# u of a feed-forward tile transposed by a round trip through DRAM and 32x32 blocks, its second product two tiles behind

## The chip, the core and the metric

The kernel runs on one core of a Trainium2 chip, in one launch. The core has a matrix engine (TensorE, PE in the profile, with its weight loads as PEld), VectorE (DVE), ScalarE (ACT), GpSimd (POOL) and SyncE (SP, which issues transfers). Each engine works its own list of instructions in order, and they meet through semaphores. The time is device microseconds of one execution; what is compared is the median over several.

## The reference

```python
# attention, for each of 8 batches and 8 heads, 576 tokens of 64 features
q_d, k_d, v_d = means of q, k, v over groups of 4 tokens
out_up    = repeat(softmax(q_d k_d^T / 8) v_d, 4)
out_local = softmax(q k^T / 8 where |i - j| < 4) v
x = (out_up + out_local) as [4608 tokens, 512]

# feed-forward
h = x @ w_in                                   # [4608, 1024]
sm = exp(h - max(h)) / (sum(exp(h - max(h))) + 1e-9)
u = h * sm
ln = (u - mean(u)) / sqrt(var(u) + 1e-6) * g_ln
out = ln @ w_out                               # [4608, 512]
```

The weights are float64 and are brought to float32 on the chip. Each float32 factor of the feed-forward products is held as a rounded high part and a remainder, and a product is made of three: high by high, high by low, low by high.

## The kernel before

**Attention** is worked batch by batch, in nine items a batch: five `Local` items (two windows of 64 keys, all heads) and four `Pooled` ones (two heads each). An item has scores with a softmax, transposes, and an output that is added to `x`. The items' scores are written one item ahead.

**The feed-forward** works tiles of 128 tokens, 36 in all, a batch behind the attention. `split_x` makes the two parts of x. `ffn_in` multiplies by `w_in` into `h`, two PSUM banks that exist once (`ps_h`, one buffer), in 24 matmuls of 128x512 (L518); then come the row's maximum (DVE, L527), the exponential (ACT, L530), the product with h and its sum (DVE, L532), the mean (POOL, L536), its subtraction in place in `e` (ACT, L539), the sum of squares (ACT, L542), and the factor `s` of a row (POOL, L544 to L557). `ffn_out` takes the result, u, whose tokens lie on partitions: in two halves of four chunks, eight PE transposes of 128x128 bring the features onto partitions (L568, into a PSUM bank), ACT rounds the high part `uh` (L571), DVE subtracts for the remainder `ul` (L573), and 24 matmuls of 128x512 with `w_out` follow (L582). ACT scales the result (L588) and issues its store (L589). `uh` and `ul` have two buffers each, one tile's worth.

**The order.** `ffn_steps` gives the feed-forward in steps, four a tile, and each attention item takes two of them. A tile's second product stands behind the first product of the next tile. A tile waits in empty steps until the batch whose x it needs is finished (`xs`). From tile 31 on (`LAST`) no attention is left, and the transposes of the tile before are put between the two halves of a first product. A planner orders the instructions of each engine from estimated durations before the program is built, taking what is ready and earliest in the program; the result is a fixed list for each engine. Two exceptions stand in the program's own order: everything that SP issues, and PE's list in the last part.

**Loads on SP** are q and k of the next batch (32 transfers at an item's start, L111), v for the pooled sums (four a batch, L131, waited for by POOL at L278), and v's windows (20, L123). A transfer whose buffer is not yet free holds back everything that SP has after it.

**The first batch** is worked among the weights: `order` writes out the steps. A weight block goes through `f32` (one ACT and four DVE instructions, L178 to L189, in a buffer of tag `osb`) and `split` (L195, L196).

Of the kernel before, what the change touches and what calls it, by code (L numbers as in the profile page):

```python
# [11 lines left out]
F32 = mybir.dt.float32  # L12
# [8 lines left out]
# High words of the float64 numbers between which float32's normal ones lie, as float32.  # L21
# [5 lines left out]
def pooled_local_attention_then_solu_ffn(  # L27
# [11 lines left out]
    P = 128  # L39
# [14 lines left out]
    # Local windows: 64 consecutive keys each; window w serves queries [qlo, qhi).  # L54
# [4 lines left out]
    # Pooled query chunks, two heads of each side by side.  # L59
# [19 lines left out]
    for half in range(2):  # L79
        m = mask[half * W:(half + 1) * W, :]  # L80
        # keep 0 where |row - col| < FAC, else -1e9
# [11 lines left out]
    # k transposed, two heads by two, block diagonal: the other head's rows stay zero  # L93
# [4 lines left out]
    # pooled q, two heads by two, block diagonal too  # L98
# [4 lines left out]
    # Partition quadrant (par, dh) gets the tokens of a 32-token block of the heads of that  # L103
    # parity, half dh of the head's features, so that transposing 32x32 blocks leaves
    # features on partitions.
# [36 lines left out]
    # A float64 comes as two words. Its float32 bits: sign and top exponent bit, the  # L142
    # next 27 bits of the high word, the top 3 bits of the low word. The high word is
    # first held to the range of float32 (read as a float32, its order is that of |w|).
    class Weights:
# [25 lines left out]
        def f32(self):  # L171
# [4 lines left out]
            t = moe.tile([P, DO], F32, tag="osb", name=f"w32_{n}", bufs=3)  # L176
# [21 lines left out]
        def w_in(self):  # L198
            for cc in range(NCC):
                for n in range(2):  # L200
                    ns = slice(n * 512, n * 512 + 512)
                    self.split(self.f32(), wi_h[:, cc, ns], wi_l[:, cc, ns])
                    yield

        # the layer norm's g goes into w_out's rows
# [13 lines left out]
    class Batch:  # L219
        """What one batch's attention holds."""  # L220
# [15 lines left out]
        # q and k transposed, with their pooled sums (the means' factors are folded into  # L236
        # the scale and the weights)
# [6 lines left out]
        def pair(self, pr):  # L244
            kT = wk.tile([P, S], F32, tag="kT", name=f"kT_{self.b}_{pr}")
# [39 lines left out]
    class FirstBatch(Batch):  # L285
        """Leaves the transposes and the sums of v to the tensor engine."""
# [77 lines left out]
    # One item of attention: scores with their softmax, then the transposes, then the output.  # L364
    class Local:
        """Two windows of the local attention, all heads."""
# [64 lines left out]
    class Pooled:  # L431
        """The pooled attention of two heads."""
# [80 lines left out]
    def ffn_in(i, xh, xl):  # L513
# [25 lines left out]
        nc.scalar.activation(e, e, AF.Identity, bias=nmu, scale=1.0)  # L539
# [3 lines left out]
        # per-token factor: r / sqrt(r^2 * m2 / DFF + 1e-6), r = 1 / (sum + 1e-9)  # L543
# [17 lines left out]
    def ffn_out(i):  # L561
        u, s = done.pop(i)
        uts = []
        for g in range(2):
            tp = ps_t.tile([P, 4, P], F32, tag="t", name=f"ut_{i}_{g}")
            for j in range(4):
                fc = 4 * g + j
                nc.tensor.transpose(tp[:, j, :], u[:, fc * P:(fc + 1) * P], ident)  # L568
            uh = moe.tile([P, 4, P], F32R, tag="uh", name=f"uh_{i}_{g}", bufs=2)
            ul = moe.tile([P, 4, P], F32R, tag="ul", name=f"ul_{i}_{g}", bufs=2)  # L570
            nc.scalar.activation(uh, tp, AF.Copy)  # L571
            latest[:] = [
                nc.vector.tensor_tensor(out=ul, in0=tp, in1=uh.bitcast(F32), op=ALU.subtract)  # L573
            ]
            uts.append((uh, ul))
# [11 lines left out]
        osb = moe.tile([P, DO], F32, tag="osb", name=f"osb_{i}", bufs=3)  # L587
# [7 lines left out]
    # The tiles from which on the last batch's attention is over.  # L595
    LAST = ((B - 1) * S) // P

    # The feed-forward's chunks, each in two halves: its first product for a tile, then
    # its second one for the tile before.
    def ffn_steps():  # L600
        split = split_x(0)
        for i in range(NTILE + 1):
            if LAST <= i < NTILE:
                # no attention is left to fill the wait for the transposed u
                first, last = ffn_in(i, *split), ffn_out(i - 1)
                next(first)
                next(last)
                yield
                yield from first
                if i + 1 < NTILE:  # L610
                    split = split_x(i + 1)
                yield from last
                continue
            if i < NTILE:
                yield from ffn_in(i, *split)
                while i + 1 < NTILE and ((i + 2) * P - 1) // S not in xs:
                    yield
                if i + 1 < NTILE:
                    split = split_x(i + 1)
            if i > 0:  # L620
                yield from ffn_out(i - 1)
# [119 lines left out]
```

## Time and profile before

| What | Value |
|---|---|
| median of 3 runs | 697.27 us (695.83 to 699.69) |
| profiled execution, span from its first to its last instruction | 695.3 us |
| PE busy (matmuls) | 658.1 us, 95% of the span |
| DVE, ACT, POOL busy | 425.7, 388.6, 316.2 us |
| moved by transfers | 57.47 MB |
| transposes of u on PE (L568) | 288 |

The profile states no time for the profiled execution beyond its span; the span is 0.5 us below the fastest run and 2.0 us below the median. Times of PE matmuls overlap, since one starts before the last has drained: what a group costs PE is read from the starts, from its first instruction to the start of what follows. In a timeline a row gives start, duration, engine, line, operation, output and input, the count of merged instructions, and in brackets the engine's idle time before it with what ended that.

### The profile page before, as it was taken

To read this page: it belongs to the slowest core of one execution; us is meant where nothing else is said; L and a number is where in the kernel's file an instruction comes from. 1 tells how busy PE (TensorE), PEld (TensorE's weight loads), DVE (VectorE), ACT (ScalarE), POOL (GpSimd) and SP (SyncE) were. 2 spreads that over 40 slices of the span, in tenths; PEclk is the share of its full clock that TensorE was granted. 3 is DMA by queue.
4 is the path that set the end of the run, shared out by engine and by line. 5 is a ranking of instruction groups with operands and counts; after the bars stand their busy time and mean duration, and the time that the engine had idled before them with its cause. 6 is when DMAs were issued, how large, how long until landed. Compare 5 with 4: busy or idle time off the path is not lost. (4 is left out here: it accounts for less than half of the span.)

```text
span 695.3 us, 12961 instructions
## 1 busy us (share of the span) xinstructions
PE 658.1 (95%) x4880; PEld 522.8 (75%) x4880; DVE 425.7 (61%) x765; ACT 388.6 (56%) x784; POOL 316.2 (45%) x509
## 2 busy tenths in 40 slices
PE   3877799989999999999999999999999999999996
PEld 2666577868877788778877788778877788778885
DVE  4899999985377555765567655665567543333232
ACT  4645666854575466635765466634756465444533
POOL 3485468574723852248423842247443732222210
PEclk9975789999999999999999999999999999999999
DMA  9957526758427521085117411184130100000000
GB/s 171 211 179 147 121 82 134 158 118 145 104 55 131 115 51 47 23 141 116 49 32 133 118 47 47 25 145 110 49 83 16 33 17 16 16 31 16 15 31 30
DMA packets 203789, 57.47 MB, mean 83 GB/s; under 512 B 187856, under 2 KB 197072, under 8 KB 203728
## 3 DMA queue, kind: packets, MB, share of 16 engines
q1 hardware_dynamic: 198544, 47.22, 33.6%
q10 hardware_dynamic: 5184, 9.44, 3.6%
q8 instruction: 38, 0.62, 0.4%
q14 instruction: 23, 0.19, 0.1%
HBM read 47.19 MB, written 9.44 MB: 81 GB/s over the span
## 5 line engine op out<-in xcount | busy, mean ns | idle before, releaser
L582 PE MATMUL o<-wo_h,uh 128*128 128x512 f32 x288 | 118.3, 411 | 1.8 <-ACT uh L571 1.4
L518 PE MATMUL h<-wi_h,xh 128*128 128x512 f32 x288 | 119.5, 415 | 0.5 <-DVE e L532 0.5
L582 PE MATMUL o<-wo_l,uh 128*128 128x512 f32 x288 | 116.1, 403 | 0.4 <-POOL wo_l L196 0.4
L518 PE MATMUL h<-wi_l,xh 128*128 128x512 f32 x288 | 115.5, 401 | 0.0
L518 PE MATMUL h<-wi_h,xl 128*128 128x512 f32 x288 | 114.6, 398 | 0.1
L527 DVE TENSOR_REDUCE nmx<-h 128x1 f32<-128x1024 f32 x36 | 43.9, 1221 | 75.0 <-PE h L518 75.0
L582 PE MATMUL o<-wo_h,ul 128*128 128x512 f32 x288 | 81.6, 403 | 1.3 <-DVE ul L573 1.3
L507 POOL TENSOR_TENSOR xl<-x,xh 128x512 fp32r<-128x512 f32 (+1 forms) x40 | 47.2, 1185 | 75.4 <-PE ut L568 41.5
L573 DVE TENSOR_TENSOR ul<-ut,uh 128x512 fp32r<-128x512 f32 x72 | 48.4, 680 | 34.3 <-ACT uh L571 33.9
L582 PEld LDWEIGHTS o<-wo_h,uh 128*128 128x128 f32 x288 | 54.6, 190 | 16.1 <-issue 2.3
L518 PEld LDWEIGHTS h<-wi_h,xh 128*128 128x128 f32 x288 | 54.4, 189 | 13.8 <-issue 2.1
L518 PEld LDWEIGHTS h<-wi_h,xl 128*128 128x128 f32 x288 | 54.3, 189 | 13.0 <-issue 0.3
L582 PEld LDWEIGHTS o<-wo_l,uh 128*128 128x128 f32 x288 | 54.8, 190 | 11.4 <-POOL wo_l L196 0.5
L518 PEld LDWEIGHTS h<-wi_l,xh 128*128 128x128 f32 x288 | 54.4, 189 | 11.2 <-issue 0.9
L582 PEld LDWEIGHTS o<-wo_h,ul 128*128 128x128 f32 x288 | 52.4, 188 | 11.9 <-DVE ul L573 1.8
L378 PE MATMUL sc<-kbd,qT 128*64 128x128 f32 x640 | 52.4, 297 | 7.4 <-ACT kbd L250 6.4
L539 ACT ACTIVATE e<-e,nmu 128x1024 f32<-128x1024 f32 x36 | 41.4, 1150 | 29.9 <-POOL nmu L536 29.9
L530 ACT ACTIVATE e<-h,nmx 128x1024 f32<-128x1024 f32 x36 | 40.1, 1114 | 30.0 <-DVE nmx L527 30.0
L398 POOL TENSOR_TENSOR pl<-pl,rsl 128x512 f32<-128x512 f32 x40 | 44.7, 1119 | 20.9 <-DVE rsl L397 20.3
L389 POOL TENSOR_TENSOR pl<-pl,mxl 128x512 f32<-128x512 f32 x40 | 43.2, 1082 | 24.0 <-DVE mxl L388 20.9
L423 PEld LDWEIGHTS xp<-plT,vw 64*64 64x64 f32 x1280 | 43.5, 143 | 13.1 <-issue 4.8
L378 PEld LDWEIGHTS sc<-kbd,qT 128*64 128x64 f32 x640 | 38.8, 145 | 19.3 <-issue 7.4
(94 smaller groups left out, 1271.7 us busy)
## 6 DMA issues: line engine op xcount, KB each, us to landing
vw<-in_v_dram SPq DMA_DIRECT2D x160, 64.0 KB
vs<-in_v_dram SPq DMA_DIRECT2D x32, 288.0 KB
out_dram<-osb ACTq DMA_DIRECT2D x36, 256.0 KB
qm<-in_q_dram SPq DMA_DIRECT2D x112, 72.0 KB
km<-in_k_dram SPq DMA_DIRECT2D x112, 72.0 KB
stage<-in_moe_w_out_dram SPq DMA_DIRECT2D x8, 512.0 KB
stage<-in_moe_w_in_dram SPq DMA_DIRECT2D x4, 512.0 KB
w<-in_moe_w_in_dram SPq DMA_DIRECT2D x4, 512.0 KB
```

Source lines behind the costliest of these rows:

```text
L378: nc.tensor.matmul(sc[wi * W:(wi + 1) * W, 2 * pr:2 * pr + 2, :], bt.qT[:, pr, s0:s0 + W], kbd[:, pr, :, s0:s0 + W], start=True, stop=True,)
L389: nc.gpsimd.tensor_tensor(out=pl, in0=pl, in1=mx.unsqueeze(2).broadcast_to([P, H, W]), op=ALU.subtract)
L398: nc.gpsimd.tensor_tensor(out=pl, in0=pl, in1=rs.unsqueeze(2).broadcast_to([P, H, W]), op=ALU.mult)
L423: nc.tensor.matmul(xp[hp, pr, qlo[w] - q0:qhi[w] - q0], bt.vw[u][hp, wi, pr, :], self.plT[hp, pr, wi * W + a0:wi * W + a0 + nw], start=Tru ...
L507: nc.gpsimd.tensor_tensor(out=xl[:, :, cs], in0=src, in1=xh[:, :, cs].bitcast(F32), op=ALU.subtract)
L518: nc.tensor.matmul(hps[:, n, :], src[:, cc, :], wt[:, cc, n * 512:(n + 1) * 512], start=(cc == 0 and src is xh and wt is wi_h), stop=(cc = ...
L527: nc.vector.tensor_reduce(out=nmx, in_=hf, op=ALU.max, axis=AX.X, negate=True)
L530: nc.scalar.activation(e, hf, AF.Exp, bias=nmx, scale=1.0, accum_out=se)
L539: nc.scalar.activation(e, e, AF.Identity, bias=nmu, scale=1.0)
L573: nc.vector.tensor_tensor(out=ul, in0=tp, in1=uh.bitcast(F32), op=ALU.subtract)
L582: nc.tensor.matmul(o, src[:, j, :], wt[:, 4 * g + j, :], start=(g == 0 and j == 0 and src is uh and wt is wo_h), stop=(g == 1 and j == 3 a ...
```

## The change

For 30 of the 36 tiles (all but 0 to 4 and 35) PE no longer transposes u. Instead:

- ACT issues a store of u, 128 rows of 4 KB, to a scratch in DRAM (three buffers), right behind the instruction that makes u.
- SP issues four loads of it (`ffn_back`), each to 32 partitions, in pieces of 1 KB, into one buffer `v` (tag `v`, a single buffer). They place a 32x32 block of u where its transpose belongs.
- DVE transposes 32x32 blocks of `v` in place, in two instructions of 128x512.
- ACT rounds `uh` from `v` rather than from PSUM, and POOL, not DVE, subtracts for `ul`.

So that a load's piece is contiguous, the columns of h are permuted: `w_in`'s columns are stored in the order (a, c, d) for feature 128c + 32a + d. The six tiles that stay on PE have ACT undo the permutation by writing u into the buffer of tag `v`. The second product stands two tiles behind the first for the 30 tiles, one behind for the six. The special order from tile 31 on is gone. To make room, the tag `osb` has two buffers instead of three and `kT` one instead of two.

```diff
-            t = moe.tile([P, DO], F32, tag="osb", name=f"w32_{n}", bufs=3)
+            t = moe.tile([P, DO], F32, tag="osb", name=f"w32_{n}", bufs=2)
...
-                    ns = slice(n * 512, n * 512 + 512)
-                    self.split(self.f32(), wi_h[:, cc, ns], wi_l[:, cc, ns])
+                    src = self.f32().rearrange("p (c a d) -> p c a d", a=4, d=32)
+                    hi, lo = (
+                        w[:, cc, :].rearrange("p (a c d) -> p c a d", a=4, d=32)[:, 4 * n:4 * n + 4]
+                        for w in (wi_h, wi_l)
+                    )
+                    self.split(src, hi, lo)
...
-            kT = wk.tile([P, S], F32, tag="kT", name=f"kT_{self.b}_{pr}")
+            kT = wk.tile([P, S], F32, tag="kT", name=f"kT_{self.b}_{pr}", bufs=1)
...
-        nc.scalar.activation(e, e, AF.Identity, bias=nmu, scale=1.0)
+        if i in ON_PE:
+
+            u = moe.tile([P, DFF], F32, tag="v", name=f"v_{i}", bufs=1)
+            nc.scalar.activation(
+                u.rearrange("p (c a d) -> p a c d", a=4, d=32),
+                e.rearrange("p (a c d) -> p a c d", a=4, d=32), AF.Identity, bias=nmu, scale=1.0,
+            )
+            e = u
+        else:
+            nc.scalar.activation(e, e, AF.Identity, bias=nmu, scale=1.0)
+        if i not in ON_PE:
+            away[i] = dram.tile([P, DFF], F32, tag="u", name=f"u_{i}")
+            nc.scalar.dma_start(away[i], e)
...
+    away = {}
+    ON_PE = (0, 1, 2, 3, 4, NTILE - 1)
+
+    def ffn_back(i):
+        if i in ON_PE:
+            return
+        d = away.pop(i)
+        v = moe.tile([P, 4, NFC, 32], F32, tag="v", name=f"v_{i}", bufs=1)
+        for a in range(4):
+            nc.sync.dma_start(
+                v[32 * a:32 * a + 32].rearrange("t b c d -> t b (c d)"),
+                d[:, 256 * a:256 * a + 256].rearrange("(b t) x -> t b x", b=4),
+            )
+        away[i] = v
...
+            else:
+                vg = v[:, :, 4 * g:4 * g + 4, :].rearrange("p b c d -> p b (c d)")
+                latest[:] = [nc.vector.transpose(vg, vg)]
+                tp = v[:, :, 4 * g:4 * g + 4, :].rearrange("p b c d -> p c b d")
+                eng = nc.gpsimd
...
             nc.scalar.activation(uh, tp, AF.Copy)
-            latest[:] = [
-                nc.vector.tensor_tensor(out=ul, in0=tp, in1=uh.bitcast(F32), op=ALU.subtract)
-            ]
+            sub = eng.tensor_tensor(out=ul, in0=tp, in1=uh.bitcast(F32), op=ALU.subtract)
...
     def ffn_steps():
         split = split_x(0)
-        for i in range(NTILE + 1):
+        left = 0
+        for i in range(NTILE + 2):
...
                 yield from ffn_in(i, *split)
+                ffn_back(i)
                 while i + 1 < NTILE and ((i + 2) * P - 1) // S not in xs:
                     yield
                 if i + 1 < NTILE:
                     split = split_x(i + 1)
-            if i > 0:
-                yield from ffn_out(i - 1)
+            while left < NTILE and left + (1 if left in ON_PE else 2) <= i:
+                yield from ffn_out(left)
+                left += 1
...
+    dram = ctx.enter_context(tc.tile_pool(name="dram", bufs=3, space=bass.MemoryType.DRAM))
```

More of the change, by code (lines that the diff above doesn't have):

```diff
@@ L559, in ffn_in @@
         yield
-    def ffn_out(i):
+    away = {}
[11 more added lines that the diff above has]
+        away[i] = v
@@ L562, in ffn_out, with ffn_ut @@
+    def ffn_ut(i):
         u, s = done.pop(i)
         uts = []
+        v = away.pop(i, None)
         for g in range(2):
[L565 to L570, printed above, removed]
@@ L571, in ffn_out @@
-            nc.scalar.activation(uh, tp, AF.Copy)
-            latest[:] = [
-                nc.vector.tensor_tensor(out=ul, in0=tp, in1=uh.bitcast(F32), op=ALU.subtract)
-            ]
-            uts.append((uh, ul))
+            if v is None:
+                tp = ps_t.tile([P, 4, P], F32, tag="t", name=f"ut_{i}_{g}")
+                for j in range(4):
+                    nc.tensor.transpose(tp[:, j, :], u[:, (4 * g + j) * P:(4 * g + j + 1) * P], ident)
+                tp = tp.rearrange("p c (b d) -> p c b d", b=4)
+                eng = nc.vector
+            else:
[3 more added lines that the diff above has]
+                eng = nc.gpsimd
@@ new lines, in ffn_ut, with ffn_out @@
+            uh = moe.tile([P, 4, 4, 32], F32R, tag="uh", name=f"uh_{i}_{g}", bufs=2)
+            ul = moe.tile([P, 4, 4, 32], F32R, tag="ul", name=f"ul_{i}_{g}", bufs=2)
+            nc.scalar.activation(uh, tp, AF.Copy)
+            sub = eng.tensor_tensor(out=ul, in0=tp, in1=uh.bitcast(F32), op=ALU.subtract)
+            if v is None:
+                latest[:] = [sub]
+            uts.append([t.rearrange("p c b d -> p c (b d)") for t in (uh, ul)])
+        return uts, s
+    def ffn_out(i):
+        uts, s = ffn_ut(i)
@@ L586, in ffn_out @@
                         )
-        osb = moe.tile([P, DO], F32, tag="osb", name=f"osb_{i}", bufs=3)
+        osb = moe.tile([P, DO], F32, tag="osb", name=f"osb_{i}", bufs=2)
         nc.scalar.activation(osb, o, AF.Copy, scale=s)
@@ L593, in pooled_local_attention_then_solu_ffn @@
     latest = []
-    LAST = ((B - 1) * S) // P
     def ffn_steps():
         split = split_x(0)
-        for i in range(NTILE + 1):
[L603 to L613, printed above, removed]
+        left = 0
+        for i in range(NTILE + 2):
             if i < NTILE:
                 yield from ffn_in(i, *split)
+                ffn_back(i)
                 while i + 1 < NTILE and ((i + 2) * P - 1) // S not in xs:
```

## The prediction

> **What bounds the kernel now.** I read first the page's busy line and its forty slices, then the table of stages.
>
> ```profile
> PE 658.1 (95%) x4880; PEld 522.8 (75%) x4880; DVE 425.7 (61%) x765; ACT 388.6 (56%) x784; POOL 316.2 (45%) x509
> ...
> PEclk9975789999999999999999999999999999999999
> ```
> ```profile
> 100.00:165.00 65.00, 58.91 (x529) 47.07 (x528) 54.30 (x101) 40.97 (x87) 42.85 (x59) 0.97 0.65 131
> 185.00:640.00 455.00, 455.00 (x3351) 357.78 (x3350) 261.21 (x483) 257.61 (x522) 198.70 (x347) 1.00 0.29 65
> 640.00:683.00 43.00, 43.00 (x198) 34.89 (x198) 14.10 (x23) 19.13 (x29) 8.06 (x26) 1.00 0.05 19
> ```
>
> The table's columns are PE, PEld, DVE, ACT, POOL, granted clock, DMA share and GB/s. From 185 us to 683 us PE has no idle time and the full clock, while DVE and ACT are at 57% and POOL at 44%. Whatever leaves PE's list there shortens the span one for one, as long as nothing new makes PE wait. Busy PE need not be dense PE, so I looked at starts: in the tail the matmuls follow each other at 0.233 us (662.84 to 663.07 below), without a gap.
>
> **What the transposes cost PE.** The starts around three sites of L568:
>
> ```profile
> 661.73 1.04 PE L568 MATMUL ut<-ident,e 128*128 128x128 f32 x8
> 662.52 0.48 PE L518 MATMUL h<-wi_h,xh 128*128 128x512 f32 x1
> 662.84 0.40 PE L518 MATMUL h<-wi_l,xh 128*128 128x512 f32 x1
> 663.07 0.40 PE L518 MATMUL h<-wi_h,xl 128*128 128x512 f32 x1
> ```
> ```profile
> 358.88 0.66 PE L568 MATMUL ut<-ident,e 128*128 128x128 f32 x4
> 359.46 0.47 PE L487 MATMUL po<-pdT,vd 72*64 72x144 f32 x4
> 359.86 0.66 PE L568 MATMUL ut<-ident,e 128*128 128x128 f32 x4
> 360.44 0.66 PE L378 MATMUL sc<-kbd,qT 128*64 128x128 f32 x8
> ```
> ```profile
> 168.04 0.60 PE L568 MATMUL ut<-ident,e 128*128 128x128 f32 x4
> 168.47 0.90 PE L443 MATMUL sd<-kd,qbd 128*96 128x144 f32 x6
> ...
> 170.38 0.66 PE L568 MATMUL ut<-ident,e 128*128 128x128 f32 x4
> 170.79 0.48 PE L582 MATMUL o<-wo_h,uh 128*128 128x512 f32 x1
> ```
>
> In the tail eight cost 0.79 us, and the matmul behind them takes 0.32 instead of 0.233 to the next start: 0.88 us a tile. Among attention it is 0.58 + 0.58 = 1.16 us at the second site and 0.43 + 0.41 = 0.84 us at the third. I take 1.0 us, the middle, for the 25 tiles from 5 to 29, and 0.88 us for the five from 30 to 34, whose transposes stand in the tail: 25.0 + 4.4 = **29.4 us less on PE**; by the ends, 30 x 0.84 = 25 to 30 x 1.16 = 35 us. Tiles 0 to 4 and 35 keep theirs.
>
> **What comes in their place, and what covers it.** The unit prices:
>
> ```profile
> L573 DVE TENSOR_TENSOR ul<-ut,uh 128x512 fp32r<-128x512 f32 x72 | 48.4, 680 | 34.3 <-ACT uh L571 33.9
> L507 POOL TENSOR_TENSOR xl<-x,xh 128x512 fp32r<-128x512 f32 (+1 forms) x40 | 47.2, 1185 | 75.4 <-PE ut L568 41.5
> L571 ACT ACTIVATE uh<-ut 128x512 fp32r<-128x512 f32 x72 | 41.7, 594 | 19.0 <-PE ut L568 18.5
> ```
> ```profile
> L246 DVE STREAM_TRANSPOSE qT<-qm 128x576 f32<-128x576 f32 x28 | 21.2, 757 | 0.0
> L278 POOL TENSOR_TENSOR vs<-vs 72x512 f32<-72x512 f32 x28 | 35.8, 1281 | 29.6 <-DMA vs<-in_v_dram 29.3
> ```
>
> DVE loses 60 subtractions of 0.68 us and gains 60 block transposes of 128x512; scaled from 0.757 us for 576 columns, 0.67 us each: 41 against 40 us, nothing. POOL gains 60 subtractions like L507: 60 x 1.185 = 71 us. Some 50 of them fall between 185 and 640 us, so POOL goes there from 199 to 258 us of about 430, 60%: room, if it is not late. ACT keeps its 60 roundings at about 0.6 us and issues 30 more stores at 0.34 us (last row below), 10 us of a queue with 40% idle. SP issues 120 loads; four of k took 2.12 us to issue (row at 381.47), so 2 us a tile. Transfers grow by 30 x 2 x 0.52 = 31 MB on 57.5 MB.
>
> Now the round trip. Rows that bound it:
>
> ```profile
> 381.47 2.12 SPq L111 DMA_DIRECT2D km<-in_k_dram  x4
> 383.69 10.63 SPq L131 DMA_DIRECT2D vs<-in_v_dram  x4
> ```
> ```profile
> 387.34 2.73 POOL L278 TENSOR_TENSOR vs<-vs 72x512 f32<-72x512 f32 x2 [1.78 <-DMA vs<-in_v_dram]
> 515.31 1.27 POOL L278 TENSOR_TENSOR vs<-vs 72x512 f32<-72x512 f32 x1 [9.28 <-DMA vs<-in_v_dram]
> ```
> ```profile
> core 0 of [0], span 695.3 us
> ...
> 692.24 0.34 ACTq L589 DMA_DIRECT2D out_dram<-osb  x1
> ```
> ```profile
> 20.00:40.00 20.00, 17.09 (x166) 14.59 (x166) 17.83 (x31) 13.22 (x36) 10.60 (x11) 0.91 0.95 226
> ```
>
> The last store, 256 KB, is issued at 692.24 us and the span ends at 695.3: 3.1 us. Another 256 KB at the best rate shown, 226 GB/s, is 1.2 us: u is in DRAM 4.3 us after its issue. The nearest read is v's, also in 1 KB pieces: 288 KB issued at 383.69 us, behind all of q and k, was there for POOL at 387.34, 3.65 us; 236 KB more make 4.7 us. From below, a read can't beat its own bytes, 2.3 us; from above, 4.7 plus the longest wait, 9.3, is 14 us. I take 4.7, so **9 us for the round trip**, up to 18.
>
> Is that covered? In the tail, where a tile takes least:
>
> ```profile
> 641.24 0.39 PE L582 MATMUL o<-wo_h,uh 128*128 128x512 f32 x1
> ...
> 646.84 0.39 PE L518 MATMUL h<-wi_h,xh 128*128 128x512 f32 x1
> ```
> ```profile
> 645.48 1.15 ACT L539 ACTIVATE e<-e,nmu 128x1024 f32<-128x1024 f32 x1 [1.57 <-POOL nmu L536]
> ```
>
> A product takes 641.24 to 646.84 = 5.6 us. u is made 646.63 - 641.24 = 5.4 us after its first product ends; with the round trip v is there at 14.4, transposed and rounded (0.67 + 0.6) at 15.7. Two tiles behind, four products stand between (the second of two tiles before, the first of the next tile, the second of the tile before, the first of the next but one), so its own second product starts at 22.4: **6.7 us to spare**, and more among attention, where items lie between as well. The single buffer v is free again when POOL has made the last `ul`, whose buffer is let go by the third of these products: 16.8 + 1.2 = 18.0, earlier than 11.2 + 5.4 + 4.3 = 20.9, when the next u can be read. So the wait costs nothing on the path. If the cover goes (18 us for the round trip), the five tiles of the tail start 2.3 us late each, 12 us.
>
> **What is queued behind the new waits.** On SP, a `ffn_back` that waits for u or for v holds back all later loads, at worst for about a tile's time. The last q and k were issued by 383.6 us (row at 381.47) and are first used by L246 at 415.57: 32 us to spare, so they bear it:
>
> ```profile
> 415.57 0.77 DVE L246 STREAM_TRANSPOSE qT<-qm 128x576 f32<-128x576 f32 x1
> ```
>
> On DVE the block transposes wait for a transfer, and the maximum and the product that free h stand behind them; ACT's rounding and POOL's subtraction wait in turn. The planner places an instruction where it expects its input: POOL's 28 additions on v, placed in that way, waited for their transfer 29.3 us in 12 waits, 2.4 us each, and PE never felt it. The free time of h:
>
> ```profile
> 376.73 1.21 DVE L532 SCALAR_TENSOR_TENSOR e<-h,e 128x1024 f32<-128x1024 f32 x1
> ```
> ```profile
> 381.10 0.40 PE L518 MATMUL h<-wi_h,xh 128*128 128x512 f32 x1
> ```
> ```profile
> DVE nmx L527 <- PE h L518: 63.3, 21, 7.9
> ```
>
> 381.10 - 377.94 = 3.2 us to spare; and DVE idles 63.3 us there for h anyway. A transpose late by 2.4 us is absorbed. I charge nothing for it and keep 0 to 1.6 us a tile for the range (two transfers late by 2.4 us each, less 3.2).
>
> **Small terms.** Tile 5's second product is put off by a tile, so one batch has 8 instead of 9 products among its items and the tail one more: 0 to 5.6 us, as far as the attention can't fill PE alone; I take 1.5. Two `osb` buffers carry 16 weight blocks:
>
> ```profile
> L189 DVE SCALAR_TENSOR_TENSOR w<-stage,w 128x512 int32<-128x512 int32 x12 | 11.5, 956 | 0.0
> L196 POOL TENSOR_TENSOR wi_l<-w,wi_h 128x512 fp32r<-128x512 f32 x8 | 11.8, 1470 | 9.6 <-ACT wi_h L195 9.6
> ```
> ```profile
> 114.91 0.63 ACT L195 ACTIVATE wo_h<-w 128x512 fp32r<-128x512 f32 x1
> ```
>
> A block keeps its buffer for at most four DVE instructions like L189, three ACT ones like L195 and POOL's: 3.8 + 1.9 + 1.5 = 7.2 us, so two buffers allow a block every 3.6 us; the last of 16 is split at 114.91 us, one every 7.2 us. I take 1 us, and 0 to 5 since the blocks come in bunches. ACT's write of u for the tiles kept on PE, the single `kT` and the end (tile 35 stays as it was) cost nothing visible.
>
> **The sum**: 695.3 - 29.4 + 1.5 + 1 = 668.4 us of span, with the 2.0 us by which the median exceeds the span, **670 us**; its own range 661 to 682.
>
> The Trainium skill speaks against the change: "VectorE: DVE Perf Modes", section "Rules for kernel authors", advises TensorE for a 128x128 transpose when PSUM will do as the target. This case's rows agree on the price alone (0.88 us on PE against 1.34 us on DVE and a round trip), but here PE is the full engine; by the rule the sum would have no gain in it and the time would stay near 697 us, which is where rival (2) ends for a reason of this kernel.
>
> **Rivals.** (1) *Partly paid back*: v is late by 3.7 us a tile on average, 0.5 us more than h's free time, 30 x 0.5 = 15 us: 685 us. For it: the wait of 9.28 us; against: 2.4 us is usual. (2) *No change*: among attention PE is full only because the order fills it, and what really paces an item is its softmax chain; then the 25.0 us taken out there come back as holes and only the tail's 4.4 us are gained: 697.3 - 4.4 + 2.5 = 695.4 us. For it: DVE, ACT and POOL wait mostly for one another and for PE, so chains are long; against: scores are written an item ahead, and PE had not one microsecond of idle time in 455. (3) *Slower*: DVE is blocked in every tile at its block transposes until store and load have landed, with the maximum and the product that free h behind them; 4.8 us late less 3.2 is 1.6 us a tile, 48 us: 670 + 48 = 718 us. It turns the sign from 4.1 us late on (0.9 us x 30 = 27 us). For it: two transfers in series, neither of which the order knows; against: nearly 7 us to spare, and DVE's idle time. (4) *It doesn't do what it says*: PE's list keeps the holes of the transposes, and only the lower price of 0.84 us a tile is gained, 25 us instead of 29.4: 675 us, inside the forecast's range.
>
> Gaps in PE's work would cost more than their length: where PE had idle time the clock was granted at 0.60 (40 to 60 us). "TensorE: Matmul & The Clock Gate", Part 1 of the Trainium skill, puts the drop at gaps above 3.4 us; a stall of 1.6 us would not reach it.
>
> ```profile
> 40.00:60.00 20.00, 16.95 (x114) 14.38 (x112) 19.59 (x35) 8.33 (x16) 15.68 (x10) 0.60 0.59 148
> ```
>
> **Chances.** Forecast with (4) 0.57; (1) 0.15; (2) 0.10; (3) 0.18. A measurement of this kernel can tell 0.5% (3.5 us) from no change: faster 0.72, same 0.10, slower 0.18. The range runs from the larger removal (30 x 1.16, no small terms: 662) to past the no-change case, 700 us, leaving out most of (3).
>
> **What would show it.** Right: no L568 group but for six tiles; PE 100% busy from 185 us to the end; the tail's period 11.2 instead of 12.09 us; POOL near 387 us; DVE unchanged; block transposes that wait under 3 us. Wrong: PE waits at h for the product on DVE or at o for ul on POOL, a block transpose idle for 4 us or more before it, SP's q and k after 415 us, or the plateau of PE starting later than 185 us.

## The result and the profile after

The changed kernel takes **700.85 us** (median of four runs, 699.26 to 702.36), the kernel before in the same comparison 696.8 us (695.83 to 699.69). The ratio is **1.006, with a 95% interval of 1.0032 to 1.0088**: 0.6% slower, where 3.9% faster was forecast. The profiled execution took 699.67 us and has a span of 697.2 us.

The busy line and the granted clock from the page of the changed kernel:

```profile
PE 640.8 (92%) x4640; PEld 506.6 (73%) x4640; DVE 421.7 (60%) x765; ACT 388.4 (56%) x784; POOL 388.9 (56%) x569
...
PEclk9975899979999999899999999999989999999999
```

PE has 240 matmuls less, as it should. DVE is at 421.7 us (425.7 before) and POOL at 388.9 (387 was forecast). So the work moved as was said, and yet the span grew by 1.9 us. The table of stages shows where (its columns are PE, PEld, DVE, ACT, POOL, granted clock, DMA share and GB/s):

```profile
265.00:350.00 85.00, 80.59 (x606) 63.46 (x606) 54.09 (x102) 47.53 (x102) 52.48 (x75) 0.96 0.55 133
350.00:435.00 85.00, 81.11 (x597) 63.44 (x594) 51.32 (x97) 51.46 (x108) 53.82 (x79) 1.00 0.55 138
435.00:520.00 85.00, 78.26 (x597) 60.93 (x596) 52.17 (x97) 48.78 (x99) 51.67 (x77) 0.96 0.57 130
520.00:600.00 80.00, 80.00 (x602) 63.44 (x600) 40.75 (x79) 44.13 (x97) 49.61 (x76) 1.00 0.38 116
...
190.00:640.00 450.00, 432.18 (x3121) 338.19 (x3122) 260.72 (x482) 255.80 (x521) 262.06 (x399) 0.98 0.50 128
```

Before, PE was busy without a break in each of these stages and the clock stood at 1.00. Now 4.4, 3.9 and 6.7 us are idle in the first three, and in two of them the clock is below 1. Over 190 to 640 us together, the last row, it is 450 - 432.2 = 17.8 us. Whoever made those holes is named by the view of the waits:

```profile
DVE v L607 <- DMA v<-u: 65.0, 26, 6.0
...
POOL vs L282 <- DMA vs<-in_v_dram: 49.8, 14, 9.4
...
ACT uh L612 <- DVE v L607: 35.3, 17, 4.8
```

VectorE stood 26 times at the new block transposes (L607), 2.5 us on average, up to 6.0 us, because the loads of u had not landed; ACT's rounding waited behind it. POOL's wait for v, 29.3 us before, is 49.8 us. None of this is PE's own wait, so one hole has to be followed. These are timeline rows of the changed kernel around 280 us, in order of time:

```profile
236.49 2.05 SPq L111 DMA_DIRECT2D qm<-in_q_dram  x4
...
245.26 0.36 ACTq L555 DMA_DIRECT2D u<-e  x1
...
253.42 2.12 SPq L111 DMA_DIRECT2D km<-in_k_dram  x4
255.63 1.87 SPq L588 DMA_DIRECT2D v<-u  x4
```
```profile
261.15 1.30 DVE L607 STREAM_TRANSPOSE v<-v 128x512 f32<-128x512 f32 x2 [6.05 <-DMA v<-u]
...
268.96 1.21 DVE L531 TENSOR_REDUCE nmx<-h 128x1 f32<-128x1024 f32 x1
...
271.43 1.10 ACT L534 ACTIVATE e<-h,nmx 128x1024 f32<-128x1024 f32 x1
...
273.86 1.30 DVE L607 STREAM_TRANSPOSE v<-v 128x512 f32<-128x512 f32 x2 [1.62 <-DMA v<-u]
...
275.09 0.73 DVE L250 STREAM_TRANSPOSE qT<-qm 128x576 f32<-128x576 f32 x1
...
277.06 1.51 DVE L399 TENSOR_SCALAR sml<-sml 128x8 f32<-128x8 f32 x1
...
278.49 1.21 DVE L536 SCALAR_TENSOR_TENSOR e<-h,e 128x1024 f32<-128x1024 f32 x1
```
```profile
279.85 0.77 PE L522 MATMUL h<-wi_h,xh 128*128 128x512 f32 x1 [4.41 <-DVE smd L459]
280.41 0.63 PE L522 MATMUL h<-wi_l,xh 128*128 128x512 f32 x1
280.84 0.63 PE L522 MATMUL h<-wi_h,xl 128*128 128x512 f32 x1
```

u's store was issued at 245.26 us, but its loads stood behind the next batch's q and k on SP and were issued at 255.63; the block transposes began at 261.15, 15.9 us after the store. DVE had been idle for 6.05 us by then, and all its work came late. One tile on it stood again for 1.62 us, and behind the two block transposes came q's, k's and a softmax step, all in the fixed list, before the product (L536) that lets go of h. (That q and k of the next batch stand there is the program's own order: `issue_after(latest[0].ins)` queues their transposes behind the latest block transposes of u.) The exponential had ended by 272.6 us; the product started at 278.49, 5.9 us later. PE waited for h from 275.4 to 279.85: the hole has 4.41 us. (The wait is put down to `smd`; the product ends at 279.70 beside it, and what PE does next is to write h.)

The hole itself is not all. After it the first products follow each other at 0.43 us (280.41 to 280.84), not 0.233. Short windows of the same trace give the granted clock behind the two longest holes, 4.41 and 4.00 us, and two more rows of PE the second of them:

```profile
280.00:285.00 5.00, 5.00 (x12) 3.98 (x13) 4.63 (x11) 3.94 (x10) 4.79 (x9) 0.50 0.39 157
505.00:510.00 5.00, 1.08 (x5) 1.08 (x6) 5.00 (x11) 4.55 (x13) 4.83 (x7) 0.71 0.00 0
510.00:515.00 5.00, 4.92 (x17) 3.82 (x17) 2.48 (x7) 3.73 (x9) 3.14 (x5) 0.61 0.14 52
```
```profile
508.92 1.75 PE L447 MATMUL sd<-kd,qbd 128*96 128x144 f32 x6 [4.00 <-ACT pd L455]
...
513.80 0.44 PE L522 MATMUL h<-wi_h,xl 128*128 128x512 f32 x1
```

The second hole comes by another way: it ends with a softmax exponential (ACT L455), whose maximum (DVE L451, 506.04 us) stood on DVE behind block transposes that had waited 1.99 us for u, q's and k's transposes, and h's maximum. That the wait for u made this hole too is read from the order, not shown.

**Where the time went.** The first instruction of the exponential of a tile is a good milestone; it divides the span into three parts.

```profile
187.15 1.11 ACT L530 ACTIVATE e<-h,nmx 128x1024 f32<-128x1024 f32 x1 [0.22 <-DVE nmx L527]
...
616.86 1.12 ACT L530 ACTIVATE e<-h,nmx 128x1024 f32<-128x1024 f32 x1 [0.23 <-DVE nmx L527]
```
```profile
192.30 1.12 ACT L534 ACTIVATE e<-h,nmx 128x1024 f32<-128x1024 f32 x1
...
619.47 1.12 ACT L534 ACTIVATE e<-h,nmx 128x1024 f32<-128x1024 f32 x1 [7.58 <-DVE nmx L531]
```

These are tile 5 and tile 30, first of the kernel before, then of the changed one. For the middle part I summed PE's rows: from the start of each row to the start of the next, less the idle time in its brackets.

| us | to tile 5 | tile 5 to 30 | of it PE idle | tile 30 to the end | span |
|---|---|---|---|---|---|
| before | 187.2 | 429.7 | 0.0 | 78.4 | 695.3 |
| after | 192.3 | 427.2 | 15.9 | 77.7 | 697.2 |

In the middle part before, u's transposes cost 25.2 us by that sum; without them, and with one second product (5.6 us) moved out to the tail, 398.9 us were to be had. It took 427.2. Of the 28.3 us between them 15.9 are idle. Another 4.7 are no loss but other matmuls: tile 30's exponential came so late that of the 24 matmuls of that second product only 4 lie behind it (596 in the middle part, 600 before), and the other 20 cost 20 x 0.233 us. The remaining 7.7 are the same matmuls at a higher price: h 149.7 us against 147.7, the scores 28.6 against 26.7, the small transposes of attention 24.5 against 20.4, the rest together 0.3 us less. The halved clock has the larger part in it, by an estimate: behind the first hole twelve products took 5.26 us (279.85 to 285.11) instead of 12 x 0.233 = 2.8 us, and behind the second PE worked from 508.92 to 513.80 us, 4.9 us, at about half the clock, so some 2.4 us too long; that is about 5 us. And 5.1 us were lost before any u had gone through DRAM, since tile 5 is the first that does.

### The profile page after: what moved, and what is told of

The parts are those of the page before. It is cut to its first block, busy times and chain, and to the rows that moved or that the text cites. A ratio compares the mean times of both kernels' runs of the same rounds, so it can differ in the third digit from the quotient of the medians.

```text
span 697.2 us, 12953 instructions
## 1 busy us (share of the span) xinstructions
PE 640.8 (92%) x4640; PEld 506.6 (73%) x4640; DVE 421.7 (60%) x765; ACT 388.4 (56%) x784; POOL 388.9 (56%) x569
## 4 chain that ended last, share of the span: by engine, by line
PE 35%; DMA 8%; SPq 7%; DVE 7%; POOL 6%; issue 5%; ACT 4%; ACTq 0%; DVEq 0%; POOLq 0%
PE o L627 14%; PE h L522 13%; DMA v<-u 4%; SPq L111 4%; SPq L588 3%; PE sc L382 2%; POOL ul L613 2%; DMA vs<-in_v_dram 2%; PE xp L427 1%; POOL vs L282 1%; PE po L491 1%; PE pdt L476 1%; DVE e L536 1%; ACT e L552 1%; DVE v L607 1%
## 5 line engine op out<-in xcount | busy, mean ns | idle before, releaser
L613 POOL TENSOR_TENSOR ul<-v,uh 128x512 fp32r<-128x512 f32 x60 | 76.9, 1283 | 32.5 <-ACT uh L612 25.8
L607 DVE STREAM_TRANSPOSE v<-v 128x512 f32<-128x512 f32 x60 | 39.3, 690 | 65.5 <-DMA v<-u 65.0
L627 PEld LDWEIGHTS o<-wo_h,uh 128*128 128x128 f32 x288 | 54.1, 188 | 17.4 <-ACT osb L633 2.7
L282 POOL TENSOR_TENSOR vs<-vs 72x512 f32<-72x512 f32 x28 | 35.9, 1283 | 49.9 <-DMA vs<-in_v_dram 49.8
L382 PE MATMUL sc<-kbd,qT 128*64 128x128 f32 x640 | 56.6, 300 | 6.8 <-ACT kbd L254 5.6
L612 ACT ACTIVATE uh<-v 128x512 fp32r<-128x512 f32 x60 | 37.3, 627 | 42.0 <-DVE v L607 35.3
L402 POOL TENSOR_TENSOR pl<-pl,rsl 128x512 f32<-128x512 f32 x40 | 44.0, 1104 | 22.1 <-DVE rsl L401 20.8
L382 PEld LDWEIGHTS sc<-kbd,qT 128*64 128x64 f32 x640 | 42.3, 148 | 19.1 <-issue 7.8
```

Source lines behind the costliest of these rows:

```text
L282: nc.gpsimd.tensor_tensor(out=vs[:, :, 0:2 * D], in0=vs[:, :, 0:2 * D], in1=vs[:, :, 2 * D:4 * D], op=ALU.add)
L382: nc.tensor.matmul(sc[wi * W:(wi + 1) * W, 2 * pr:2 * pr + 2, :], bt.qT[:, pr, s0:s0 + W], kbd[:, pr, :, s0:s0 + W], start=True, stop=True,)
L402: nc.gpsimd.tensor_tensor(out=pl, in0=pl, in1=rs.unsqueeze(2).broadcast_to([P, H, W]), op=ALU.mult)
L607: latest[:] = [nc.vector.transpose(vg, vg)]
L613: sub = eng.tensor_tensor(out=ul, in0=tp, in1=uh.bitcast(F32), op=ALU.subtract)
L627: nc.tensor.matmul(o, src[:, j, :], wt[:, 4 * g + j, :], start=(g == 0 and j == 0 and src is uh and wt is wo_h), stop=(g == 1 and j == 3 a ...
```

## The experiments

Two theories stood at the start. *A*: the round trip is late for the place that the fixed order gives to what needs it, and DVE's list, waiting there, makes PE's holes. *B*: the holes come from something else in the change, above all from POOL's 71 us more (*B1*) or from the rearranged order. Later ones split A by the side that is late and looked for the lost start. Unless a run says otherwise, its edit is made on the changed kernel.

### The round trip left out

```diff
-            away[i] = dram.tile([P, DFF], F32, tag="u", name=f"u_{i}")
-            nc.scalar.dma_start(away[i], e)
...
-        d = away.pop(i)
...
-            nc.sync.dma_start(
-                v[32 * a:32 * a + 32].rearrange("t b c d -> t b (c d)"),
-                d[:, 256 * a:256 * a + 256].rearrange("(b t) x -> t b x", b=4),
-            )
...
-    ON_PE = (0, 1, 2, 3, 4, NTILE - 1)
+    ON_PE = (0, 1, 2, 3, 4)
...
-                latest[:] = [nc.vector.transpose(vg, vg)]
+                ug = u.rearrange("p (b c d) -> p b c d", b=4, d=32)[:, :, 4 * g:4 * g + 4, :]
+                latest[:] = [nc.vector.transpose(vg, ug.rearrange("p b c d -> p b (c d)"))]
```

No store and no loads of u: DVE transposes the 32x32 blocks from e into v, so the blocks are turned but not moved to their partitions. All else of the new order stays.

> The changed kernel without the round trip: DVE transposes the 32x32 blocks straight from the buffer in which u was made into v, with no store of u and no loads (tile 35 goes this way too, instead of PE; the blocks are not the ones a full transpose needs, so the result is another). Everything else, POOL's subtraction and the distance of two tiles among it, stays. Theory A (DVE, and ACT and POOL behind it, wait in their fixed order for transfers that land later than planned; PE then runs dry): the 65 us of DVE's waits for v vanish, PE's idle time between 190 and 680 us falls from 16 us to under 4, its clock stays full, and the time falls to 670 to 682 us. Rival B (the new order and the load on POOL make the holes, transfers or not): PE keeps 10 us or more of idle time and the time stays above 692 us.

Measured: **675.48 us** (672.59 to 676.18), ratio 0.9689 (0.9662 to 0.9716). The row of 190 to 640 us and the waits of the block transposes (L598 here):

```profile
190.00:640.00 450.00, 449.62 (x3247) 354.89 (x3244) 273.15 (x499) 268.24 (x541) 274.59 (x420) 1.00 0.30 66
```
```profile
DVE v L598 <- POOL ul L604: 20.6, 11, 3.2
...
DVE v L598 <- ACT e L552: 14.4, 7, 4.3
```

PE is idle for 0.4 us of 450 with the clock at 1.00. From tile 5 to tile 30 it takes 399.1 us; with the 17 matmuls of a second product that lie behind tile 30's exponential here, 400.5 were to be had (429.7 - 25.2 - 17 x 0.233): the removal pays in full. DVE still waits 35 us at the transposes, for POOL and ACT, and PE hardly feels it; POOL is as busy as in the changed kernel (392.6 us). So the round trip costs 700.85 - 675.48 = 25.4 us (some 0.9 us of it is tile 35, which is off PE here too), nearly the whole gain that was forecast. B falls. That it is DVE's place in the order, and not the transfers as such, is not shown by this run alone, which takes both away. What is left is 192.7 us to tile 5.

### All tiles transposed on PE, in the new order

```diff
-    ON_PE = (0, 1, 2, 3, 4, NTILE - 1)
+    ON_PE = range(NTILE)
```

> The changed kernel with all 36 tiles transposed on PE: no scratch, no block transposes, no subtraction on POOL, second product one tile behind; what stays is the smaller buffers, the permuted columns, the single buffer for u and the lost special order of the tail. The tail should cost 5 x 1.4 us more (PE waits for the rounded u between transposes and product). Theory C (some 5 us of the loss come from these side edits in the first 190 us): 705 to 712 us, the tile-5 first product at 190 us or later. Without C: 700 to 705 us.

Measured: **711.45 us** (710.01 to 713.45), ratio 1.0207 (1.0182 to 1.0232). PE is idle for 0.6 us between 190 and 640. This kernel has the work of the kernel before, the smaller buffers, ACT's permuted write and no special order at the end, and these cost 15 us against 696.16 us of the kernel before in that comparison. Something in the change beside the transposes is thus dear, and that isn't the round trip.

### POOL's subtraction given back to DVE

```diff
-                eng = nc.gpsimd
+                eng = nc.vector
```

> The changed kernel with the remainder ul subtracted on DVE for all tiles, as before the change, so that POOL is rid of 71 to 77 us. Theory A (late transfers at the head of DVE's list): no gain, DVE gets 41 us more work behind the same waits, 699 to 710 us. Rival B1 (POOL's added load makes the holes): 680 to 692 us.

Measured: **704.97 us** (703.36 to 707.93), ratio 1.0138 (1.0107 to 1.0168). POOL is back at 335.1 us, DVE at 459.0, and DVE still waits 67.7 us for u's loads. POOL's load isn't what makes the holes; B1 falls, and the move of the subtraction to POOL gained some 4 us.

### The q and k loads spread

```diff
             if n == 0 and b + 1 < B:
                 nxt = Batch(b + 1)
-                for pr in range(NPR):
-                    nxt.load_q_k(pr)
+            if n < NPR and nxt is not None:
+                nxt.load_q_k(n)
```

The 32 transfers are given to SP at four items' starts, eight at each, not all at the first.

> The changed kernel with the next batch's q and k issued in four portions of 8 transfers, at items 0 to 3, instead of 32 at item 0, so that a load of u waits on SP behind 4 us of issues instead of 17. If the late loads of u come from SP's queue (A, first half): the waits of 5 to 6 us at block transposes go, DVE's waits for v fall from 65 to about 45 us, and the time falls by 4 to 10 us, to 690 to 697. If they come from the length of the round trip itself (A, second half) or if B holds: no change, 698 to 703 us.

Measured: **694.29 us** (ten runs, 690.92 to 698.59), ratio 0.9973 (0.9947 to 0.9999). The time is 6.6 us below the changed kernel's, but not by the way that was expected: DVE's wait for u did not fall, it rose.

```profile
DVE v L607 <- DMA v<-u: 83.6, 26, 11.0
POOL vs L282 <- DMA vs<-in_v_dram: 37.2, 17, 6.5
```

The loads of u were issued sooner, 3.7 us after their store instead of 5.3 (mean of tiles 5 to 29), and yet DVE stood longer at them: it reached the block transposes earlier still. PE's idle time between 190 and 640 us is 13.9 us (17.8 in the changed kernel), and POOL's wait is shorter too. So SP's queue is a part of the delay, but why the time fell is not shown, and shorter waits on DVE are not the reason. The next run moves DVE's place instead.

### The block transposes behind the next tile's product

```diff
-        nc.vector.scalar_tensor_tensor(
+        stt[i] = nc.vector.scalar_tensor_tensor(
...
-                latest[:] = [nc.vector.transpose(vg, vg)]
+                with tc.issue_after(stt[i + 1].ins):
+                    latest[:] = [nc.vector.transpose(vg, vg)]
```

The planner may place a tile's block transposes only behind the product with h of the tile after it. Then the product that frees the next tile's h can't stand behind this tile's late transfer. No other instruction is given a new condition, and SP's list stays as it is.

> The changed kernel with tile i's block transposes queued on DVE behind the product that frees h of tile i+1: the wait is later in DVE's order, when the load has landed. Theory A: DVE's waits for v fall under 25 us, no stall of PE on h of more than 1.5 us is left, and the time falls to 672 to 690 us. Rival B: 697 us or more, since the order gets only tighter.

Measured: **689.45 us** (685.4 to 691.18), ratio 0.9889 (0.9852 to 0.9927).

```profile
POOL vs L282 <- DMA vs<-in_v_dram: 54.1, 13, 11.2
...
DVE v L609 <- DMA v<-u: 16.4, 7, 4.2
PE plt L411 <- POOL pl L402: 9.5, 5, 3.4
```

DVE's wait falls from 65.0 to 16.4 us and the time by 11.4 us, by the order alone. PE's waits for the product with h are down to 0.4 us in one wait, as theory A had it. What is left now shows at POOL: it stands 54.1 us for v's loads, up to 11.2 us, and PE waits for the softmax product (L402) that POOL has behind them.

### Both, and POOL's additions moved in the same way

The two edits above together:

> Both edits together: q and k issued in four portions, and tile i's block transposes queued on DVE behind the product that frees h of tile i+1. Theory A: the two causes of lateness add up, DVE's waits for v under 15 us, the time 680 to 687 us. If the gain of the first was chance or the second already holds it: 688 to 692 us.

Measured: **683.37 us** (681.91 to 684.0), ratio 0.9819 (0.98 to 0.9839). DVE's wait for u is 2.2 us; POOL's for v still 40.0, and PE's longest hole, 5.2 us, ends with a softmax product on POOL (L464). Then POOL's additions on v, both of each group of heads, were taken out of `pooled_vc` and put behind the softmax product of the next item:

```diff
         def pooled_vc(self, c, hs):
-            vs = load_vs(self.b, c, hs)
...
+            self.vs.append((c, hs, load_vs(self.b, c, hs)))
+
+        def pooled_add(self, behind):
+            with tc.issue_after(behind.ins):
+                for c, hs, vs in self.vs:
...
+            self.vs = []
...
-            nc.gpsimd.tensor_tensor(
+            self.mul = nc.gpsimd.tensor_tensor(
                 out=pl, in0=pl, in1=rs.unsqueeze(2).broadcast_to([P, H, W]), op=ALU.mult
             )
...
+            if n in (3, 4):
+                cur.pooled_add(items[n].mul)
```

> The kernel of the two edits together, and POOL's additions for the pooled v of a load queued behind the softmax product of the item after, so that POOL too does not stand waiting for a load. Theory A, taken to POOL: its waits for v's loads fall from about 50 to under 20 us, PE's idle time between 190 and 640 us to under 5 us, the time 674 to 682 us. If POOL's waits cost PE nothing: the same as with two edits.

Measured: **674.04 us** (673.76 to 681.75), **ratio 0.9724 (0.9662 to 0.9785)**: faster than both kernels.

```profile
190.00:640.00 450.00, 447.16 (x3226) 352.89 (x3225) 269.67 (x495) 266.74 (x539) 271.28 (x414) 1.00 0.54 134
```
```profile
POOL vs L287 <- DMA vs<-in_v_dram: 26.8, 14, 5.8
...
DVE v L615 <- DMA v<-u: 4.4, 3, 3.1
```

u goes through DRAM as in the changed kernel, with as much traffic (134 against 128 GB/s), and POOL is as busy (389.9 us). But PE is idle for 2.8 us instead of 17.8, and the clock is 1.00. So it isn't the traffic as such that made the holes. Nor did u come sooner: from a tile's store to its block transposes it takes 13.4 us on average here (tiles 5 to 29), and 10.2 us in the changed kernel. Of theory A's numbers one was missed: POOL's wait is 26.8 us, not under 20. Three of the four runs took 674 us and one 681.75. The ratio can't be told from that of the kernel without a round trip (0.9689, 0.9662 to 0.9716), and in that kernel the two moves on DVE and POOL could have won little more, since PE was idle for 0.4 us there: **waited for at the right place, the late transfer cost nothing that these times can tell.**

The three waits and idle times side by side, each from the same rows of its kernel:

| us | DVE waits for u | POOL waits for v | PE idle, 190 to 640 | median |
|---|---|---|---|---|
| changed kernel | 65.0 | 49.8 | 17.8 | 700.85 |
| loads spread | 83.6 | 37.2 | 13.9 | 694.29 |
| transposes behind the next product | 16.4 | 54.1 | 13.8 | 689.45 |
| both | 2.2 | 40.0 | 8.2 | 683.37 |
| both, and POOL's additions | 4.4 | 26.8 | 2.8 | 674.04 |
| no round trip | none | 33.9 | 0.4 | 675.48 |

### The smaller buffers, alone

The kernel before, with two `osb` buffers and one `kT`, and nothing else:

```diff
-            t = moe.tile([P, DO], F32, tag="osb", name=f"w32_{n}", bufs=3)
+            t = moe.tile([P, DO], F32, tag="osb", name=f"w32_{n}", bufs=2)
...
-            kT = wk.tile([P, S], F32, tag="kT", name=f"kT_{self.b}_{pr}")
+            kT = wk.tile([P, S], F32, tag="kT", name=f"kT_{self.b}_{pr}", bufs=1)
...
-        osb = moe.tile([P, DO], F32, tag="osb", name=f"osb_{i}", bufs=3)
+        osb = moe.tile([P, DO], F32, tag="osb", name=f"osb_{i}", bufs=2)
```

> The kernel before with only the two buffer counts of the change: the tag osb with two buffers instead of three, kT with one instead of two. Theory C1 (the 5 us lost in the first 190 us come from these buffers, through the weight blocks): the exponential of tile 5 at 191 to 193 us instead of 187, the time 700 to 703 us. If they come from the permuted columns or the single buffer for u: 695 to 698 us.

Measured: **707.77 us** (706.76 to 709.38), ratio 1.0175 (1.0153 to 1.0197): 12 us, for what the prediction had priced at 1, and more than the 700 to 703 us expected here. It is also most of the 15 us of the kernel with all tiles on PE. Each of the two alone, first `kT`:

> The kernel before, with one buffer for kT instead of two and nothing else. The two smaller buffers together made the kernel before 1.75% slower (about 12 us): 5 us by the fifth tile and the rest behind it. Theory S1 (each has its own part: osb the start, where the weights are split, kT every batch behind it): start of tile 5's exponential within 1.5 us of before (187.2), then 5 to 6 us lost between tiles 5 and 30, 702 to 704 us, ratio 1.007 to 1.010. Rival S2 (all of it is kT, whose next transposes wait for the block copies of the last pair): 707 us, with 4 to 5 us lost already by tile 5. Rival S3 (all of it is osb): 697 us, ratio within 0.003 of 1.

Measured: 705.23 us (704.71 to 705.74), ratio 1.0114 (1.0073 to 1.0155). Then `osb`:

> The kernel before, with two buffers of tag osb instead of three (weight blocks at the start, results of the second product later) and nothing else. S1: tile 5's exponential starts 3 to 5 us late and nothing more is lost, 701 to 703 us, ratio 1.005 to 1.008. S2: 697 us, ratio within 0.003 of 1. S3: 707 us, with some 5 us lost by tile 5 and some 6 us behind it, where the scaled results wait for their stores.

Measured: 707.46 us (707.09 to 707.82), ratio 1.0146 (1.0112 to 1.018). By the three parts of the span:

| us | to tile 5 | tile 5 to 30 | tile 30 to the end | span |
|---|---|---|---|---|
| before | 187.2 | 429.7 | 78.4 | 695.3 |
| one `kT` | 187.4 | 437.6 | 78.5 | 703.5 |
| two `osb` | 198.6 | 429.0 | 78.4 | 706.0 |
| both | 192.1 | 435.4 | 78.5 | 706.0 |
| without round trip | 192.7 | 399.1 | 79.0 | 670.8 |
| spread, moved, POOL's additions | 191.5 | 401.4 | 79.3 | 672.2 |

Theory S1 has the places right (`osb` at the start, `kT` behind it) and both sizes too small: 11.4 us where 3 to 5 were expected, and 7.9 where 5 to 6 were. And they do not add up: together they lose less at the start than `osb` alone.

`osb` is plain in the trace. These are rows of the weights with two buffers, ACT's and one of POOL's (L178 takes a buffer, L195 is the last but one to use it, POOL's L196 the last):

```profile
85.99 0.64 ACT L178 ACTIVATE w<-stage 128x512 f32<-128x512 f32 x1
88.65 0.67 ACT L178 ACTIVATE w<-stage 128x512 f32<-128x512 f32 x1
...
99.07 0.62 ACT L195 ACTIVATE wo_h<-w 128x512 fp32r<-128x512 f32 x1
...
100.80 1.76 POOL L196 TENSOR_TENSOR wo_l<-w,wo_h 128x512 fp32r<-128x512 f32 x1
...
102.77 0.66 ACT L178 ACTIVATE w<-stage 128x512 f32<-128x512 f32 x1
...
126.56 0.66 ACT L195 ACTIVATE wo_h<-w 128x512 fp32r<-128x512 f32 x1
```

The buffer taken at 85.99 us comes free when POOL has made the remainder, at 102.56, and the next block starts at 102.77; that of 88.65 us is held until then too. A block holds its buffer for 16.6 us, not the 7.2 us of its own instructions; on DVE its four instructions lie spread from 88.18 to 97.17 us, with attention and feed-forward work among them. The last block is split at 126.56 us against 114.91 before, 11.65 us late, and tile 5 is 11.4 us late. In the changed kernel it is split at 123.88.

For `kT` PE stays full (449.4 of 450 us from 190 on), but the same score matmuls come in 56 uninterrupted groups instead of 38 between tiles 5 and 30 and cost 31.4 us instead of 26.7; the rest of the 7.9 us lies mainly in h (1.8) and u's transposes (1.5). That the finer order is the cause is argued, not shown. In the kernel with POOL's additions moved, which has one `kT` too, the scores come in 41 groups and cost 26.8 us: there nothing of it is seen.

### A third `osb` buffer back

The kernel with all three moves, with `osb` at three again; the room comes from the small factors of a row:

```diff
-    small = ctx.enter_context(tc.tile_pool(name="small", bufs=4))
+    small = ctx.enter_context(tc.tile_pool(name="small", bufs=3))
...
-            t = moe.tile([P, DO], F32, tag="osb", name=f"w32_{n}", bufs=2)
+            t = moe.tile([P, DO], F32, tag="osb", name=f"w32_{n}", bufs=3)
...
-        osb = moe.tile([P, DO], F32, tag="osb", name=f"osb_{i}", bufs=2)
+        osb = moe.tile([P, DO], F32, tag="osb", name=f"osb_{i}", bufs=3)
```

> The kernel with the q and k loads spread, the block transposes behind the next tile's product and POOL's additions on v behind the next item's (674.0 us), with three buffers of tag osb again; the room comes from three instead of four buffers for the small per-row factors. If two osb buffers cost this kernel the 4 to 5 us by which all changed kernels reach tile 5 late, its exponential of tile 5 starts at 187 to 188 us instead of 191.5 and the time is 669 to 671 us, the time that was forecast for the change (670), ratio 0.960 to 0.964. Rival: the delay at the start belongs to the permuted write of u and the second products' new places, not to osb; then tile 5 stays at 190 to 192 us and the time at 673 to 675 us. A third: three buffers of small factors hold something back, 675 us or more with idle time of PE between 190 and 640 us.

Measured: **672.24 us** (666.41 to 674.65), ratio 0.9641 (0.9577 to 0.9705); the profiled execution took 670.06 us.

```profile
185.95 1.12 ACT L540 ACTIVATE e<-h,nmx 128x1024 f32<-128x1024 f32 x1
...
588.80 1.11 ACT L540 ACTIVATE e<-h,nmx 128x1024 f32<-128x1024 f32 x1 [3.93 <-DVE nmx L537]
```

Tile 5 starts at 185.9 us, 5.6 us earlier than with two buffers, and earlier than expected: the lost start is `osb`'s, as far as the small factors' buffers, changed along with it, have no part in it. From tile 5 to tile 30 it takes 402.9 us, 1.5 us more. The time is a little above the 669 to 671 us expected. Its interval overlaps with that of the kernel with two buffers (0.9662 to 0.9785), so by the times the two can't be told apart; the two profiled executions differ by 4.4 us of span, but the four times of this kernel alone lie up to 8.2 us apart.

## Why the prediction was wrong

The forecast of 670 us was 31 us too low. Step by step:

- **What bounds the kernel, and what the transposes cost: right.** PE set the end. 1.0 us a tile was taken for the 25 tiles among attention; the rows of PE give 25.2 us in that part. Without the round trip that part is shorter by 30.6 us: these 25.2, 4.0 of the 17 matmuls that move behind it, and 1.4 by which all the rest is shorter. In the tail of the changed kernel the first products start 11.20 us apart (634.13, 645.33 and 656.53 us), as forecast.
- **The loads moved to other engines: right.** DVE 421.7 against 425.7 us, POOL 388.9 where 387 was expected, and neither is the cause.
- **The price of the round trip: right where nothing stands before it.** In the tail of the changed kernel:

```profile
634.71 0.33 ACTq L555 DMA_DIRECT2D u<-e  x1
...
637.50 1.73 SPq L588 DMA_DIRECT2D v<-u  x4
642.00 1.30 DVE L607 STREAM_TRANSPOSE v<-v 128x512 f32<-128x512 f32 x2 [0.84 <-DMA v<-u]
```

  Store to loads 2.8 us, loads to transposes 4.5 us: 7.3 us, where 9 was taken (4.3 and 4.7). Among attention it was 10.2 us on average (tiles 5 to 29) and 15.9 us in the case above (245.26 to 261.15), inside the 18 kept as the upper end. The step on SP had asked only whether q and k bear to stand behind `ffn_back`; it did not ask what `ffn_back` itself stands behind, which is 19 us of q's and k's issues (236.49 to 255.5) once a batch.
- **"Is that covered?": the step that failed first.** The 6.7 us to spare were counted to the second product that needs u. But the wait is where the planner puts the block transposes in DVE's list, not where their result is needed: DVE stood at them 65.0 us in 26 waits, and 16.4 us when they were moved behind the next product. Cover that lies behind the waiting instruction does not help what is queued there with it.
- **"A transpose late by 2.4 us is absorbed. I charge nothing": the step that cost the forecast.** The mean wait was 2.5 us, as was taken. But lateness does not come evenly, nor does it go away: after 6.05 us in one tile DVE's list was still behind when the next 1.62 us came, and with two transposes of u, those of q and k and a softmax step in front, the product that frees h started 5.9 us after the exponential it needs, against 3.2 us of free time. In all it gave 15.9 us of holes between tiles 5 and 30, and 7.7 us of dearer matmuls. Rival (3) had this mechanism, at 48 us, and rival (1) at 15 us; the measured cost of the round trip is 25.4 us. That it had cost PE nothing before, when POOL stood 29.3 us for v, was taken as evidence for both engines; the runs show the limit of that: at 40.0 us of such waits the time fell from 683.37 to 674.04 us when the additions were moved, while 33.9 us cost nothing visible without the round trip.
- **Small terms: wrong in size.** One us was taken for `osb` (0 to 5 kept) and nothing for `kT`. By themselves they cost 11 and 9 us in the medians, 12 together; in the changed kernel 5.1 us are lost at the start. The buffer's time was estimated from the work done in it, 7.2 us, and is 16.6 us with what stands between (two buffers, 85.99 to 102.56 us).
- **The chances.** The sign came from the round trip's waits (25.4 us, where the sum had nothing) and the start (5.1 us, where it had 1) together. Without the round trip, and with the start as it is, the forecast of 670 us would have been 5.5 us low.

On the clock, the prediction had set the gaps at 1.6 us and expected no drop. The rows above show 0.50 and 0.61 behind holes of 4.41 and 4.00 us, while 350 to 435 us, whose longest hole is 1.82 us, stays at 1.00. But the experiments show the drop behind much shorter holes too. These rows are of the kernel with the third `osb` buffer:

```profile
342.60 0.69 PE L482 MATMUL pdt<-ident,pd 96*72 96x96 f32 x6 [1.58 <-POOL pd L470]
```
```profile
344.00:346.00 2.00, 2.00 (x9) 1.85 (x8) 1.23 (x1) 0.81 (x2) 1.64 (x3) 0.50 0.71 194
```

With the transposes behind the next product, holes of 2.01 us (to 263.06 us) and 2.22 us (to 273.72) were followed by 0.50 as well, from 264.3 to 267.6 us and from 274.6 to 277.8. "TensorE: Matmul & The Clock Gate", Part 1 of the Trainium skill, puts the drop at gaps above 3.4 us; the changed kernel's trace alone would agree, these don't, and the measurement decides: a stall of 1.6 us can cost clock.

The Trainium skill's rule against the change ("VectorE: DVE Perf Modes", "Rules for kernel authors": TensorE for a 128x128 transpose) would have left the time near 697 us. The changed kernel's time is near that, but for another reason; with the waits moved, the same transposes on DVE give 674.04 us. Where PE is the full engine the measurement decides against the rule.

What stays open: what makes up the rest of the 7.7 us of dearer matmuls beside the clock's 5 or so; why the spread loads shortened the time though DVE stood longer; why a hole of 1.58 us drew the clock down and one of 1.82 us did not; why one `kT` costs 7.9 us in the order of the kernel before and nothing visible in the last ones; and why the two buffers together lose less at the start than `osb` alone.

## What to carry to other kernels

Where an engine works a fixed list, time to spare has to be counted at the instruction that waits, and what matters is what stands behind it in that list: placed behind the instructions that must not be late, the same round trip cost nothing here that the times can tell. When the work that keeps an engine full is taken out, waits elsewhere that cost nothing before must be priced anew. And a buffer taken away is priced by the time that it is held in the trace, from its first writer to its last reader, not by the work done in it.

## What the runs showed of the hardware

A hole of 4.41 us in PE costs more than its length: behind it the clock was granted at 0.50 and twelve products of 128x512 took 5.26 instead of 2.8 us, so it cost 6.9 us. Shorter holes can cost too: the clock was at 0.50 for about 3.3 us behind holes of 1.58, 2.01 and 2.22 us, and back at 1.00 after that (346.8 to 350 us for the first), while one of 1.82 us left it at 1.00. And the trip of 512 KB through DRAM, from the issue of the store to the first instruction on the loaded data, took 7.3 us with an idle queue and 15.9 us where 32 loads of 72 KB were being issued on the queue of the loads.
